# Talking-heads attention with a gated MLP: the row maxima and reciprocal sums of two softmax groups taken in shared instructions

## Chip, cores and metric

The kernel runs on one core of a Trainium2 chip. The metric is the time of one execution in device microseconds (us); lower is better. Engines are named as in the profile: PE is TensorE (PEld its weight loads), DVE VectorE, ACT ScalarE, POOL GpSimd, SP the engine that issues most transfers.

## What is computed

The inputs are q, k, v of shape (4 batches, 12 heads, 448 positions, 64), two 12x12 head-mixing matrices, and the weights of a gated MLP. Cut to what matters, with float32 throughout:

```python
scores = q @ k.transpose(0, 1, 3, 2) / sqrt(64)
scores = einsum('bhij,hg->bgij', scores, w_pre)           # mix heads before the softmax
attn = exp(scores - max(scores, -1))
attn = attn / (sum(attn, -1) + 1e-9)
attn = einsum('bhij,hg->bgij', attn, w_post)              # mix heads after it
x = (attn @ v).transpose(0, 2, 1, 3).reshape(4, 448, 768)
h = gelu(x @ w_in); u, v = halves of h
v = layer_norm(v) * g_ln; v = w_sg @ v + b_sg             # mixes positions
out = x + (u * v) @ w_out
```

## The kernel before, in words

**Groups.** The queries of a batch are cut into four chunks of 120, 120, 120 and 88. A group is 10 query rows of a chunk with all 12 heads, that is 120 rows laid on the partitions, with the 448 key positions along the free dimension. There are 12, 12, 12 and 9 groups in a batch's chunks, 180 in all. Two neighbouring groups of a chunk make a pair: 88 pairs have two groups, and one pair in each batch's fourth chunk has one, so that there are 92 pairs. The second and the fourth chunk of a batch run backwards, from their last group to their first.

**The way of a pair.** The scores of a chunk (`qk`, L643) are evacuated to SBUF (L302, L669), written to DRAM by SP and read back pair by pair (`load_pair`, L740), so that the heads of ten queries lie on the partitions. `premix` (L745) multiplies by the first mixing matrix on PE: 8 fp32 matmuls for the first chunk, 12 fp16 ones (high and low parts) for the others, for both groups of the pair in turn. Each group's result lies in a PSUM tile of its own, one bank of 2 KB a partition, from the pool `ps_s2` with two buffers.

**The way of a group.** `slot` (L863) then runs each group by itself: the row maximum with its sign turned (`softmax_max`, L775, DVE, reads PSUM); the exponential with its row sum (`softmax_exp`, L782, ACT, reads PSUM, and a second ACT instruction that reads out the sum); the reciprocal of the sum (`norm_r`, L787 and L788, two DVE instructions on one column); then, for the 45 groups of batch 0 ("full" groups), the second mixing matrix scaled by the reciprocal (`w_norm`, tile `wp`, one or two POOL instructions), and 8 fp32 matmul passes of PE (`postmix`, L830). For the 135 others, p is scaled (`p_norm`), split into an fp16 high part (`p_hi`) and low part (`p_lo`), mostly on POOL, and multiplied with the second mixing matrix in fp16 (L840). `postmix` writes into one bank of the two-bank tile `at2`; the result is evacuated (`postmix_hi`, L855, by the helper at L302) to SBUF. `av` (L951) multiplies with v, and the MLP units (L983 and around) follow as PE has room. p lies in one of three buffers (`p32p`), freed by the `postmix` of a full group and by `p_lo` otherwise.

**What sets the order.** The order in which every engine runs its instructions is written out in advance by a planner (`Plan`, L187) with a clock for each engine. Each step is a generator that yields engine, cost in ns, a rank, the time at which its input is there, and conditions on buffers; `run` (L239) takes the step that can start first, by rank among those within 100 ns of it. A result counts as usable 200 ns after its step ends (`LAT`). Engines with several possible places for a step (`p_norm`, evacuations) are chosen by the planner's clocks. Ranks are group numbers with offsets: `premix` n-3.5, maximum n-3, exponential n-2.5, reciprocal n-2, `postmix` n. The next `premix` is allowed once both exponentials of the pair before are planned (L768). Engines run their instructions in this order without overtaking; the planned times are estimates and the real waits are those of semaphores.

**Other users of the two banks.** In the start, `tr_bank` (L1296) gives transposes a bank of `at2` and a tile of `ps_s2` in turn. In the last batch `any_bank` (L1005) lets the MLP's units use the banks of `ps_s2` and `at2` beside its own two.

Of the kernel before, what the change touches and what calls it, by code (L numbers as in the profile page):

```python
# [9 lines left out]
F32 = mybir.dt.float32  # L10
# [3 lines left out]
AF = mybir.ActivationFunctionType  # L14
ALU = mybir.AluOpType
AX = mybir.AxisListType
PSUM = bass.MemoryType.PSUM
# [63 lines left out]
def talking_heads_gmlp(ctx, tc, q, k, v, w_pre, w_post, w_in, g_ln, w_sg, b_sg, w_out, out):  # L81
    nc = tc.nc
    B, H, S, D = q.shape
# [3 lines left out]
    P = 128  # L87
# [36 lines left out]
    p32p = ctx.enter_context(tc.tile_pool(name="p32p", bufs=3))  # L124
    wpp = ctx.enter_context(tc.tile_pool(name="wpp", bufs=2))
    dram = ctx.enter_context(tc.tile_pool(name="dram", bufs=1, space=DRAM))
    ps_s2 = ctx.enter_context(tc.tile_pool(name="ps_s2", bufs=2, space=PSUM))
    ps_at = ctx.enter_context(tc.tile_pool(name="ps_at", bufs=1, space=PSUM))
    ps_wk = ctx.enter_context(tc.tile_pool(name="ps_wk", bufs=2, space=PSUM))
    ps_ml = ctx.enter_context(tc.tile_pool(name="ps_ml", bufs=2, space=PSUM))  # L130
# [14 lines left out]
    wpc_hi = const.tile([P, H * NH], F16, name="wpc_hi")  # L145
    wpc_lo = const.tile([P, H * NH], F16, name="wpc_lo")
    at2 = ps_at.tile([P, 2, 512], F32, name="at2")
    p_ring = [[const.tile([P, (NC - 1) * TC + P], F16, name=f"p{w}{i}") for i in range(3)] for w in "hl"]
    neg_half = const.tile([P, 1], F32, name="neg_half")
    wv_hi = const.tile([P, KK, DH], F16, name="wv_hi")  # L150
# [36 lines left out]
    class Plan:  # L187
# [22 lines left out]
        def past(self, name, n):  # L210
            return 0 if n < 0 else self.tm.get((name, n))

        @staticmethod
        def after(times):
            return None if None in times else max(times)
# [78 lines left out]
    pl = Plan()  # L294
# [450 lines left out]
    def premix(p):  # L745

        i, t, n = pairs_[p]
        g = gring[p % RING]  # L750
        ns = sorted((m for m in range(n, min(n + 2, NG)) if pair_of[m] == p), key=lambda m: glist[m][2])
        for m in sorted(ns):
            st[m] = {"s2": ps_s2.tile([P, 512], F32, tag="s2", name="ps_s2")}
        if i < N_Q32:
            terms = (wpre32, g_full(p)),
        else:
            terms = (wpre_hi, g[:, :, 0]), (wpre_hi, g[:, :, 1]), (wpre_lo, g[:, :, 0])
        for k, (w, x) in enumerate(terms):
            for u, m in enumerate(ns):
                for f in range(2):  # L760
                    o, rows = 64 * (f ^ u), slice(64 * f, 64 * f + NH * H)
                    nc.tensor.matmul(st[m]["s2"][o:o + 64, :S], lhsT=w[rows], rhs=x[rows, u, :],  # L762
                                     start=(k == 0), stop=(k == len(terms) - 1))
        return sorted(ns)

    def all_premix():
        for p, (i, _, n) in enumerate(pairs_):
            t = yield "pe", 1500 if i < N_Q32 else 570, n - 3.5, 0, lambda: after([seen(("pair", p)), past("exp", n - 1), past("exp", n - 2)])  # L768
            for m in premix(p):
                tm["pre", m] = t  # L770
                pl.add(slot(m, t))

    def softmax_max(n):
        nm = small.tile([P, 1], F32, tag="nm", name="nm")
        nc.vector.tensor_reduce(out=nm, in_=st[n]["s2"][:, :S], axis=AX.X, op=ALU.max, negate=True)  # L775
        st[n]["nm"] = nm

    def softmax_exp(n):
        x = st[n]
        x["p32"] = p32p.tile([P, S], F32, tag="p32", name="p32")  # L780
        x["ss"] = small.tile([P, 1], F32, tag="ss", name="ss")
        nc.scalar.activation(out=x["p32"], in_=x["s2"][:, :S], func=AF.Exp, bias=x["nm"], accum_out=x["ss"])  # L782

    def norm_r(n):
        x = st[n]
        x["rs"] = small.tile([P, 1], F32, tag="rs", name="rs")
        nc.vector.tensor_scalar(out=x["rs"], in0=x["ss"], scalar1=1e-9, scalar2=1.0 / S_P, op0=ALU.add, op1=ALU.mult)  # L787
        nc.vector.reciprocal(out=x["rs"], in_=x["rs"])  # L788

    def w_norm(n):  # L790
        x = st[n]
# [71 lines left out]
    def slot(n, t):  # L863
        b, c, _ = glist[n]
        i = NCH * b + ORD.index(c)
        t = yield "dve", 531, n - 3, t
        softmax_max(n)
        t = yield "act", 611, n - 2.5, t, lambda: after([past("exp", n - 1), past("p32", n - 3)])
        softmax_exp(n)
        tm["exp", n] = t  # L870
        t = yield "dve", 300, n - 2, t, lambda: past("r", n - 1)
        norm_r(n)
        tm["r", n] = t
        full = n < N_F32 and (n < N_FULL or n * P_F32 % 1 < P_F32 or ck["pe"] < max(ck["dve"], ck["pool"]) + C_F32)
        if full:
            t = yield None, W_NORM[n < N_W], n - 1, t, lambda: after([past("ph", n - 1), past("post", n - 2)])
# [128 lines left out]
    def any_bank(b):  # L1005


        pool, tag = ps_ml, "ml"
        if b == B - 1:
            spare[0] += 1  # L1010
            pool, tag = ((ps_ml, "ml"), (ps_s2, "s2"), (None, "at"))[spare[0] % 3]
        if tag == "ml":
            name = bank()
        else:
            name = f"{tag}{spare[0] // 3 % 2}"
            if tag == "at":
                k = spare[0] // 3 % 2
                return name, lambda: at2[:, k]
        return name, lambda: pool.tile([P, 512], F32, tag=tag, name="ps_x")

    def gelu(ps, rows, cols, out, view, ml, done, need, last=True):

# [230 lines left out]
    with tc.manual_schedule():  # L1253
# [41 lines left out]

        def tr_bank():  # L1296
            turns[0] += 1
            if turns[0] % 2 == 0:
                return ps_s2.tile([P, 512], F32, tag="s2", name="ps_tr")
            return at2[:, turns[0] // 2 % 2]  # L1300

        def turned(part, e):
            src, oh, ol = part
# [123 lines left out]
```

## Time and profile before

| what | us |
|---|---|
| median of 3 runs | 637.63 |
| lowest and highest of them | 634.28, 639.41 |
| the profiled execution: its own time | 637.85 |
| the profiled execution: its span, first to last instruction | 636.1 |

Times in the rows below are us from the span's start, unless marked ns. "A <- B" in a row of waits says that A's engine sat idle until B ended. A row of the timeline has the start, the duration, the engine, the line, the operation and its tiles, and in square brackets the engine's idle time before it with what ended it; a number with x behind it counts merged instructions, and then the duration runs from the first one's start to the last one's end. PEclk is the granted clock of TensorE as a share of its full 2.4 GHz.

### The profile page before, as it was taken

The numbers are of one execution on the slowest core, as the hardware profiler recorded it, in microseconds if no ns is written. First come the engines' busy times: TensorE is split into PE (matmuls) and PEld (weight loads), VectorE is DVE, ScalarE is ACT, GpSimd is POOL, SyncE is SP. The second block draws the span as 40 slices with busy tenths as digits, with TensorE's granted clock in tenths as the row PEclk, the third lists the DMA queues.
The fourth block names the chain that finished last, engine by engine and source line by source line (L and its number), as shares of the span: only waits on it lengthen the run. The fifth ranks groups of instructions, "written<-read, shape, count | busy, mean of one in ns | idle before, by whom it ended". The sixth has DMA issues, their size and how long they took to land.

```text
span 636.1 us, 22960 instructions
## 1 busy us (share of the span) xinstructions
PE 587.2 (92%) x9305; PEld 389.0 (61%) x9305; DVE 451.8 (71%) x1093; ACT 451.8 (71%) x1038; POOL 385.4 (61%) x557
## 2 busy tenths in 40 slices
PE   7777879779999899999999999999999999999997
PEld 3234647557665665766676665667566746677764
DVE  5747678794899888676779979665788787544570
ACT  5646567666858779798769769787888778876332
POOL 4213553477577968786667968664697677866000
PEclk9878999989999699999999999999899999999999
DMA  9899498787488875769488747575697456440002
GB/s 220 230 254 304 125 285 212 187 219 195 125 247 252 210 185 145 195 178 268 126 246 205 203 111 192 150 201 163 181 239 214 130 149 170 134 113 4 3 1 88
DMA packets 79412, 112.22 MB, mean 176 GB/s; under 512 B 29290, under 2 KB 65802, under 8 KB 79306
## 3 DMA queue, kind: packets, MB, share of 16 engines
q1 hardware_dynamic: 79046, 110.74, 64.5%
q8 instruction: 73, 1.20, 0.8%
q14 instruction: 33, 0.27, 0.1%
q10 hardware_dynamic: 260, 0.01, 0.0%
HBM read 66.00 MB, written 44.73 MB: 174 GB/s over the span
## 4 chain that ended last, share of the span: by engine, by line
PE 57%; DVE 16%; ACT 9%; DMA 8%; issue 5%; POOL 4%; SPq 0%; POOLq 0%; ACTq 0%; DVEq 0%
PE ps_x L983 9%; PE ps_av L951 9%; PE ps_s L762 7%; PE ps_u L983 6%; PE ps_qk L643 6%; PE ps_v L983 6%; PE at L840 5%; PE at L830 4%; DVE s L669 4%; DVE nm L775 4%; ACT at L302 2%; ACT p L782 2%; DMA q<-in_q_dram 2%; DMA xTl<-in_moe_w_in_dram 2%; ACT s L302 2%
## 5 line engine op out<-in xcount | busy, mean ns | idle before, releaser
L302 ACT ACTIVATE at<-at 112x480 f32<-112x480 f32 x179 | 110.1, 616 | 43.7 <-PE at L830 23.2
L307 POOL TENSOR_TENSOR pl<-p,ph 128x448 f16<-128x448 f32 x127 | 133.4, 1054 | 8.7 <-ACT ph L302 4.2
L782 ACT ACTIVATE p<-ps_s,nm 128x448 f32<-128x448 f32 x180 | 114.1, 635 | 26.5 <-DVE nm L775 25.9
L775 DVE TENSOR_REDUCE nm<-ps_s 128x1 f32<-128x448 f32 x180 | 105.3, 615 | 31.6 <-PE ps_s L762 30.4
L669 DVE SCALAR_TENSOR_TENSOR s<-ps_qk,s 120x448 f16<-120x448 f32 (+1 forms) x172 | 100.5, 615 | 18.0 <-ACT s L302 16.3
L304 POOL TENSOR_SCALAR p<-p,rs 128x448 f32<-128x448 f32 x87 | 56.4, 649 | 66.1 <-DVE rs L788 27.5
L302 ACT ACTIVATE s<-ps_qk 120x448 f16<-120x448 f32 (+2 forms) x158 | 79.0, 544 | 12.2 <-PE ps_qk L643 10.4
L643 PE MATMUL ps_qk<-kT,qT 64*128 64x448 f16 (+1 forms) x576 | 79.0, 362 | 7.5 <-DVE s L669 2.6
L840 PEld LDWEIGHTS <-ph 64*128 64x128 f16 x2160 | 53.7, 94 | 40.2 <-issue 24.6
L951 PE MATMUL ps_av<-at,v 112*64 112x120 f32 (+1 forms) x1536 | 77.4, 260 | 0.7 <-ACT at L302 0.7
L951 PEld LDWEIGHTS ps_av<-at,v 112*64 112x64 f32 x1536 | 74.0, 137 | 4.3 <-issue 1.8
L304 POOL TENSOR_SCALAR wp<-wpost,rs 128x60 f32<-128x60 f32 (+1 forms) x64 | 27.2, 436 | 72.4 <-DVE rs L788 53.7
L830 PE MATMUL at<-wp,p 128*112 128x120 f32 x360 | 50.5, 288 | 20.6 <-ACT at L302 10.0
L983 PE MATMUL ps_u<-xTh,wbuf 128*128 128x128 f16 (+1 forms) x768 | 66.9, 217 | 0.4 <-DVE gbuf L1039 0.4
L840 PE MATMUL at<-wpc_hi,ph 64*128 64x60 f16 x1080 | 62.0, 190 | 5.5 <-ACT at L302 4.7
L983 PEld LDWEIGHTS <-wbuf 128*128 128x128 f16 x1152 | 60.5, 100 | 7.4 <-issue 5.7
L830 PEld LDWEIGHTS at<-wp,p 128*112 128x112 f32 x360 | 43.0, 189 | 34.1 <-POOL wp L304 17.1
L304 POOL TENSOR_SCALAR ph<-p 128x448 f16<-128x448 f32 x89 | 50.8, 571 | 18.3 <-ACT xTh L302 6.8
L983 PE MATMUL ps_u<-xTl,wbuf 128*128 128x128 f16 (+1 forms) x384 | 61.8, 216 | 0.0
L840 PE MATMUL at<-wpc_hi,pl 64*128 64x60 f16 x1080 | 60.6, 188 | 0.8 <-DVE rs L787 0.5
L840 PE MATMUL at<-wpc_lo,ph 64*128 64x60 f16 x1080 | 61.0, 188 | 0.0
L983 PE MATMUL ps_x<-wo,gbuf 128*128 128x384 f16 (+1 forms) x336 | 56.6, 328 | 0.0
(214 smaller groups left out, 1176.5 us busy)
## 6 DMA issues: line engine op xcount, KB each, us to landing
g<-s_d SPq DMA_DIRECT2D x176, 210.0 KB, 4.4
s_d<-s SPq DMA_DIRECT2D x62, 420.0 KB, 3.9
s_d<-s SPq DMA_DIRECT2D x24, 336.0 KB, 3.4
v<-in_v_dram SPq DMA_DIRECT2D x12, 448.0 KB, 7.3
out_dram<-ot SPq DMA_DIRECT2D x24, 192.0 KB, 2.9
q<-in_q_dram SPq DMA_DIRECT2D x11, 384.0 KB, 5.3
st<-in_k_dram SPq DMA_DIRECT2D x9, 448.0 KB, 5.0
st<-in_moe_w_out_dram SPq DMA_DIRECT2D x8, 384.0 KB, 4.3
```

The costliest lines, as they stand in the source:

```text
L302: e.activation(out=o, in_=i, func=AF.Copy, scale=scale)
L304: e.tensor_scalar(out=o, in0=i, scalar1=scale, scalar2=1.0, op0=ALU.mult, op1=ALU.mult)
L307: (e or pl.on).tensor_tensor(out=o, in0=a, in1=b, op=ALU.subtract)
L643: nc.tensor.matmul(ps[:rows, :S], lhsT=qT2[i % 2][r, tq, h // 2, :rows], rhs=kT[r, h // HG, tk, h // 2 % 2, :], start=(n == 0), stop=(n == 2))
L669: nc.vector.scalar_tensor_tensor(out=e[:ev, h % 2, 1, :], in0=ps[:ev, :S], scalar=1.0 / math.sqrt(D), in1=e[:ev, h % 2, 0, :], op0=ALU.mul ...
L762: nc.tensor.matmul(st[m]["s2"][o:o + 64, :S], lhsT=w[rows], rhs=x[rows, u, :], start=(k == 0), stop=(k == len(terms) - 1))
L775: nc.vector.tensor_reduce(out=nm, in_=st[n]["s2"][:, :S], axis=AX.X, op=ALU.max, negate=True)
L782: nc.scalar.activation(out=x["p32"], in_=x["s2"][:, :S], func=AF.Exp, bias=x["nm"], accum_out=x["ss"])
L830: nc.tensor.matmul(ps[:TC, jc * w:(jc + 1) * w], lhsT=x["p32"][:, jc * TC:(jc + 1) * TC], rhs=x["wp"], start=True, stop=True)
L840: nc.tensor.matmul(at2[:, hf ^ glist[n][2] % 2, jc * w:(jc + 1) * w], lhsT=l[rows, js], rhs=r[rows], start=(k == 0), stop=(k == 2))
L951: nc.tensor.matmul(ps[a * D:(a + 1) * D, k3 * rows:(k3 + 1) * rows], lhsT=x[:, h, jc, :], rhs=y[:, jc, h, w:w + rows], start=(jc == 0 and ...
L983: nc.tensor.matmul(o, lhsT=l, rhs=r, start=first, stop=last)
```

## The change

The two score tiles of a pair become the two banks of one tile `s2`, which is allotted once. One DVE instruction takes the maxima of both groups (128 partitions x 2 x 448 in, 128 x 2 out), after `premix` of the pair. Two exponentials follow as before, each with its own column of the maxima and of the sums. The addition with its scaling, and the reciprocal, are then done once for the pair on two columns, after the second exponential; only then do the two groups go their own ways in `slot`. The planner's costs are 60 + 475 ns a group for the maxima, 635 for an exponential (611 before) and 270 for the reciprocals of the pair (300 a group before). `tr_bank` and `any_bank` use the banks of `s2`.

```diff
--- before.py
+++ after.py
@@ -124,7 +124,7 @@
     p32p = ctx.enter_context(tc.tile_pool(name="p32p", bufs=3))
     wpp = ctx.enter_context(tc.tile_pool(name="wpp", bufs=2))
     dram = ctx.enter_context(tc.tile_pool(name="dram", bufs=1, space=DRAM))
-    ps_s2 = ctx.enter_context(tc.tile_pool(name="ps_s2", bufs=2, space=PSUM))
+    ps_s2 = ctx.enter_context(tc.tile_pool(name="ps_s2", bufs=1, space=PSUM))
     ps_at = ctx.enter_context(tc.tile_pool(name="ps_at", bufs=1, space=PSUM))
     ps_wk = ctx.enter_context(tc.tile_pool(name="ps_wk", bufs=2, space=PSUM))
     ps_ml = ctx.enter_context(tc.tile_pool(name="ps_ml", bufs=2, space=PSUM))
@@ -145,6 +145,7 @@
     wpc_hi = const.tile([P, H * NH], F16, name="wpc_hi")
     wpc_lo = const.tile([P, H * NH], F16, name="wpc_lo")
     at2 = ps_at.tile([P, 2, 512], F32, name="at2")
+    s2 = ps_s2.tile([P, 2, 512], F32, name="s2")
     p_ring = [[const.tile([P, (NC - 1) * TC + P], F16, name=f"p{w}{i}") for i in range(3)] for w in "hl"]
     neg_half = const.tile([P, 1], F32, name="neg_half")
     wv_hi = const.tile([P, KK, DH], F16, name="wv_hi")
@@ -749,8 +750,8 @@
         i, t, n = pairs_[p]
         g = gring[p % RING]
         ns = sorted((m for m in range(n, min(n + 2, NG)) if pair_of[m] == p), key=lambda m: glist[m][2])
-        for m in sorted(ns):
-            st[m] = {"s2": ps_s2.tile([P, 512], F32, tag="s2", name="ps_s2")}
+        for u, m in enumerate(ns):
+            st[m] = {"u": u}
         if i < N_Q32:
             terms = (wpre32, g_full(p)),
         else:
@@ -759,33 +760,38 @@
             for u, m in enumerate(ns):
                 for f in range(2):
                     o, rows = 64 * (f ^ u), slice(64 * f, 64 * f + NH * H)
-                    nc.tensor.matmul(st[m]["s2"][o:o + 64, :S], lhsT=w[rows], rhs=x[rows, u, :],
+                    nc.tensor.matmul(s2[o:o + 64, u, :S], lhsT=w[rows], rhs=x[rows, u, :],
                                      start=(k == 0), stop=(k == len(terms) - 1))
         return sorted(ns)
 
     def all_premix():
         for p, (i, _, n) in enumerate(pairs_):
             t = yield "pe", 1500 if i < N_Q32 else 570, n - 3.5, 0, lambda: after([seen(("pair", p)), past("exp", n - 1), past("exp", n - 2)])
-            for m in premix(p):
-                tm["pre", m] = t
-                pl.add(slot(m, t))
-
-    def softmax_max(n):
-        nm = small.tile([P, 1], F32, tag="nm", name="nm")
-        nc.vector.tensor_reduce(out=nm, in_=st[n]["s2"][:, :S], axis=AX.X, op=ALU.max, negate=True)
-        st[n]["nm"] = nm
-
-    def softmax_exp(n):
-        x = st[n]
-        x["p32"] = p32p.tile([P, S], F32, tag="p32", name="p32")
-        x["ss"] = small.tile([P, 1], F32, tag="ss", name="ss")
-        nc.scalar.activation(out=x["p32"], in_=x["s2"][:, :S], func=AF.Exp, bias=x["nm"], accum_out=x["ss"])
-
-    def norm_r(n):
-        x = st[n]
-        x["rs"] = small.tile([P, 1], F32, tag="rs", name="rs")
+            ns = premix(p)
+            tm.update({("pre", m): t for m in ns})
+            pl.add(pair_slot(p, ns, t))
+
+    def pair_slot(p, ns, t):
+
+        a = min(ns)
+        x = {}
+        for k in ("nm", "ss", "rs"):
+            x[k] = small.tile([P, 2], F32, tag=k, name=k)[:, :len(ns)]
+        t = yield "dve", 60 + 475 * len(ns), a - 3, t
+        nc.vector.tensor_reduce(out=x["nm"], in_=s2[:, :len(ns), :S], axis=AX.X, op=ALU.max, negate=True)
+        for n in sorted(ns):
+            t0 = yield "act", 635, n - 2.5, t, lambda: after([past("exp", n - 1), past("p32", n - 3)])
+            u = st[n]["u"]
+            st[n]["p32"] = p32p.tile([P, S], F32, tag="p32", name="p32")
+            nc.scalar.activation(out=st[n]["p32"], in_=s2[:, u, :S], func=AF.Exp, bias=x["nm"][:, u:u + 1],
+                                 accum_out=x["ss"][:, u:u + 1])
+            tm["exp", n] = t0
+        t = yield "dve", 270, a - 2, t0
         nc.vector.tensor_scalar(out=x["rs"], in0=x["ss"], scalar1=1e-9, scalar2=1.0 / S_P, op0=ALU.add, op1=ALU.mult)
         nc.vector.reciprocal(out=x["rs"], in_=x["rs"])
+        for n in sorted(ns):
+            st[n]["rs"] = x["rs"][:, st[n]["u"]:st[n]["u"] + 1]
+            pl.add(slot(n, t))
 
     def w_norm(n):
         x = st[n]
@@ -863,14 +869,6 @@
     def slot(n, t):
         b, c, _ = glist[n]
         i = NCH * b + ORD.index(c)
-        t = yield "dve", 531, n - 3, t
-        softmax_max(n)
-        t = yield "act", 611, n - 2.5, t, lambda: after([past("exp", n - 1), past("p32", n - 3)])
-        softmax_exp(n)
-        tm["exp", n] = t
-        t = yield "dve", 300, n - 2, t, lambda: past("r", n - 1)
-        norm_r(n)
-        tm["r", n] = t
         full = n < N_F32 and (n < N_FULL or n * P_F32 % 1 < P_F32 or ck["pe"] < max(ck["dve"], ck["pool"]) + C_F32)
         if full:
             t = yield None, W_NORM[n < N_W], n - 1, t, lambda: after([past("ph", n - 1), past("post", n - 2)])
@@ -1005,18 +1003,16 @@
     def any_bank(b):
 
 
-        pool, tag = ps_ml, "ml"
+        tag = "ml"
         if b == B - 1:
             spare[0] += 1
-            pool, tag = ((ps_ml, "ml"), (ps_s2, "s2"), (None, "at"))[spare[0] % 3]
+            tag = ("ml", "s2", "at")[spare[0] % 3]
         if tag == "ml":
             name = bank()
         else:
-            name = f"{tag}{spare[0] // 3 % 2}"
-            if tag == "at":
-                k = spare[0] // 3 % 2
-                return name, lambda: at2[:, k]
-        return name, lambda: pool.tile([P, 512], F32, tag=tag, name="ps_x")
+            k = spare[0] // 3 % 2
+            return f"{tag}{k}", lambda: (s2 if tag == "s2" else at2)[:, k]
+        return name, lambda: ps_ml.tile([P, 512], F32, tag=tag, name="ps_x")
 
     def gelu(ps, rows, cols, out, view, ml, done, need, last=True):
 
@@ -1295,9 +1291,7 @@
 
         def tr_bank():
             turns[0] += 1
-            if turns[0] % 2 == 0:
-                return ps_s2.tile([P, 512], F32, tag="s2", name="ps_tr")
-            return at2[:, turns[0] // 2 % 2]
+            return (s2, at2)[turns[0] % 2][:, turns[0] // 2 % 2]
 
         def turned(part, e):
             src, oh, ol = part
```

## Rows read from the trace of the kernel before

**Rows 1.** The page, part 1: busy time, share of the span, instructions.
```profile
span 636.1 us, 22960 instructions
...
PE 587.2 (92%) x9305; PEld 389.0 (61%) x9305; DVE 451.8 (71%) x1093; ACT 451.8 (71%) x1038; POOL 385.4 (61%) x557
```

**Rows 2.** Windows: busy us of PE, PEld, DVE, ACT, POOL; PEclk, DMA share, GB/s.
```profile
25.00:170.00 145.00, 118.98 (x1207) 81.78 (x1203) 102.95 (x267) 91.13 (x218) 69.34 (x120) 0.92 0.81 221
170.00:300.00 130.00, 123.59 (x2122) 80.46 (x2122) 107.97 (x255) 105.42 (x242) 100.76 (x130) 0.96 0.75 204
300.00:578.00 278.00, 270.90 (x5220) 182.43 (x5215) 202.26 (x502) 221.68 (x518) 200.99 (x265) 0.99 0.63 170
578.00:636.00 58.00, 54.57 (x654) 36.44 (x652) 24.28 (x42) 19.23 (x35) 6.65 (x13) 1.00 0.07 25
```

**Rows 3.** The page, part 4: the chain that ended last.
```profile
PE 57%; DVE 16%; ACT 9%; DMA 8%; issue 5%; POOL 4%; SPq 0%; POOLq 0%; ACTq 0%; DVEq 0%
PE ps_x L983 9%; PE ps_av L951 9%; PE ps_s L762 7%; PE ps_u L983 6%; PE ps_qk L643 6%; PE ps_v L983 6%; PE at L840 5%; PE at L830 4%; DVE s L669 4%; DVE nm L775 4%; ACT at L302 2%; ACT p L782 2%; DMA q<-in_q_dram 2%; DMA xTl<-in_moe_w_in_dram 2%; ACT s L302 2%
```

**Rows 4.** Groups of DVE instructions, shapes apart: xcount | busy us, mean ns.
```profile
L775 DVE TENSOR_REDUCE nm<-ps_s 128x1 f32<-128x448 f32 x180 | 105.3, 615 | 31.6 <-PE ps_s L762 30.4
...
L788 DVE RECIPROCAL rs<-rs 128x1 f32<-128x1 f32 x180 | 29.5, 164 | 6.2
...
L787 DVE TENSOR_SCALAR rs<-ss 128x1 f32<-128x1 f32 x180 | 26.5, 147 | 28.1 <-ACT p L782 26.8
...
L1033 DVE SCALAR_TENSOR_TENSOR gl_a<-gl_a,ps_v 128x512 f32<-128x512 f32 x12 | 8.2, 686 | 10.0 <-ACT gl_a L1030 9.8
...
L1033 DVE SCALAR_TENSOR_TENSOR gl_a<-gl_a,ps_v 128x256 f32<-128x256 f32 x4 | 1.6, 411 | 0.5 <-ACT gl_a L1030 0.5
```

**Rows 5.** Waits from 25 to 170 us: total us, times, longest us.
```profile
POOL wp L304 <- DVE rs L788: 53.7, 23, 12.1
...
PEld at L830 <- POOL wp L304: 17.1, 14, 3.2
...
PE at L830 <- ACT at L302: 9.1, 12, 1.8
PE at L830 <- POOL wp L304: 8.8, 7, 2.8
...
PEld ps_s L762 <- ACT p L782: 5.1, 4, 2.0
```

**Rows 6.** Timeline, one pair of groups: start us, us, instruction.
```profile
66.38 1.16 DVE L775 TENSOR_REDUCE nm<-ps_s 128x1 f32<-128x448 f32 x2 [2.20 <-PE ps_s L762]
...
68.11 0.16 DVE L788 RECIPROCAL rs<-rs 128x1 f32<-128x1 f32 x1
68.27 0.62 ACT L782 ACTIVATE p<-ps_s,nm 128x448 f32<-128x448 f32 x1
...
68.47 1.02 POOL L304 TENSOR_SCALAR wp<-wpost,rs 128x60 f32<-128x60 f32 x2 [4.14 <-DVE rs L788]
...
69.39 0.16 DVE L788 RECIPROCAL rs<-rs 128x1 f32<-128x1 f32 x1
...
69.59 1.05 PE L830 MATMUL at<-wp,p 128*112 128x120 f32 x8 [1.55 <-POOL wp L304]
69.75 0.63 POOL L304 TENSOR_SCALAR wp<-wpost,rs 128x120 f32<-128x120 f32 x1 [0.26 <-DVE rs L788]
...
70.67 0.57 ACT L302 ACTIVATE at<-at 112x480 f32<-112x480 f32 x1 [0.36 <-PE at L830]
...
71.39 1.04 PE L830 MATMUL at<-wp,p 128*112 128x120 f32 x8 [0.75 <-ACT at L302]
```

**Rows 7.** Timeline from 53 us: two postmixes and their first evacuation.
```profile
53.69 1.86 PE L830 MATMUL at<-wp,p 128*112 128x120 f32 x16
...
55.59 0.58 ACT L302 ACTIVATE at<-at 112x480 f32<-112x480 f32 x1 [0.86 <-PE at L830]
```

**Rows 8.** Timeline of the start: turning keys and queries.
```profile
7.37 0.61 DVE L307 TENSOR_TENSOR kT<-ps_tr,kT 128x448 f16<-128x448 f32 x1
...
7.89 0.49 PE L324 MATMUL ps_tr<-ident,q 128*128 128x128 f32 x3
```

## Prediction

> **What bounds the kernel now.** I read the page's busy shares first, then windows by stage, then the chain, then the waits of the stage in which PE idles. DVE is busy for 71% of the span, PE for 92% [rows 1]. The windows show where the other 8% lie [rows 2]: PE is idle for 145 - 119.0 = 26.0 us between 25 and 170 us (batch 0, the full groups), but only 6.4 of 130 us from there to 300, 7.1 of 278 us to 578, and 3.4 us in the tail, which has no softmax. From 170 us on, then, the end is set by PE's own work, and a faster DVE can win back at most some 13 us there. The chain agrees: 57% of it is PE and 16% DVE, of which the row maximum is 4% of the span, about 25 us [rows 3]. In the first stage PE waits mostly for the softmax chain: 17.1 + 8.8 = 25.9 us in 21 waits for `wp`, the mixing weights scaled by the reciprocal, and POOL in turn sits 53.7 us waiting for that reciprocal; 9.1 us more go to waits for an evacuation of `at2` [rows 5].
>
> **The maxima.** 180 DVE instructions of 615 ns become 88 on two banks and 4 on one. The trace has no two-bank reduction. From PSUM, 512 columns take 686 ns and 256 take 411 [rows 4], a slope of 1.07 ns a column, so the double one should take 0.615 + 448 x 1.07 ns = 1.10 us. Two back to back take 1.16 us today [rows 6], two apart 1.23. Its ends are 0.615 us (the second bank free) and 1.23 us (nothing shared); per pair that is a relief of 0.55 us down to a loss of 0.07, for 88 pairs 48 us to -6 us of DVE time. I take 1.10, the slope of the nearest rows: 88 x 0.06 = 5 us.
>
> Those rows say that little is left to save: in the back-to-back pair the second maximum adds 1.16 - 0.615 = 0.545 us, of which 448 x 1.07 = 0.48 is the columns themselves [rows 4, 6]. The Trainium skill (Perfetto Trace Analysis, Optimizing Scalar/DVE Operations) puts the engine-busy overhead of a DVE instruction on PSUM at about 125 ns. By that figure the 88 dropped instructions would give 11 us of DVE time, by the rows 5; the sum goes by the rows.
>
> **The reciprocals.** 360 instructions become 184: 88 pairs of instructions of 147 + 164 ns [rows 4] go, 88 x 0.311 = 27 us of DVE time. The second column should cost a nanosecond or so by the slope above; at the other end, two columns for the price of two instructions, nothing is saved. I take 27. DVE's relief is then 5 + 27 = 32 us of 451.8, to about 420 us (66% of the span).
>
> **What reaches the end.** Little of it, because PE is full where most of the groups run. If 32 of 452 us left the chain's DVE share evenly, 16% of 636 = 102 us would lose 102 x 0.07 = 7 us. PE's idle time from 170 us on is 13.5 us in all, and PE's own work takes over where a DVE stretch leaves the chain; I count half of the 7, 3.5 us. The planner sees a DVE clock that is 2 x (531 + 300) - (1010 + 270) = 382 ns lighter a pair and an ACT clock 48 ns heavier, so it may hand a few evacuations to DVE; I cost that at nothing, since ACT and POOL are busy for some 80% or less of the windows [rows 2]. Where they were needed, it would cost up to the DVE time just won.
>
> **What comes later.** The first group of a pair now waits for its partner twice: its exponential starts 1.10 - 0.615 = 0.5 us later, and its reciprocal comes after the second exponential. In the pair shown, the first reciprocal starts at 68.11 and the second at 69.39 [rows 6]: 1.28 us later for the first group, about nothing for the second. Queued behind the waiting reciprocal on DVE are evacuations of the scores and pieces of the weights' preparation; for `wp` POOL waits, for that PE. From 170 us on PE has other work; in batch 0 it hasn't always. The same rows show what comes back. PE's postmix of the first group waits for `wp` until 69.59; the second group's `wp` is ready at 70.38, but its postmix starts at 71.39, just after the first one's evacuation (70.67 to 71.24). The other case is two postmixes back to back, after which the first evacuation starts only at 55.59 although the pair of postmixes began at 53.69 and half of the 1.86 us would have done [rows 7]. Writes to one bank of `at2` and reads of the other thus never overlap here; the order planned decides who waits. With both groups released by one reciprocal, their scaled weights come one `wp` apart (0.63 and 1.02 us in these rows), no more than a postmix takes, and the planner should put the two postmixes back to back. The first would then start near 70.6 instead of 69.59 and the second end near 72.5, against 71.39 + 1.04 = 72.43 now. So +0.1 us a pair, and for batch 0's 23 pairs between -0.6 (where the evacuation's wait goes and the delay is hidden by a matmul of another kind) and +1.28 us each, or -14 to +29 us. I take 0 to +2, say +1 us.
>
> **One tile for two banks.** The lesson of `at2` holds for `s2`: a `premix` may not write one bank while the other is read. But the planner lets it start only after both exponentials, and its matmuls take both groups in turn, so waiting for the second instead of the first moves it by no more than PE waits here today, 5.1 us in 4 waits [rows 5]; I count 0, at most +5. In the start, the second transpose into the pool's tiles at 7.89 would wait for the reader of the first, which ends at 7.98 [rows 8]: +0.1 us. In the tail `s2`'s two banks alternate with four others, so the earlier one is read out by then; 0.
>
> **The sum.** 637.85 (the profiled execution, whose 1.75 us outside the span stay) - 3.5 + 1 + 0.1 = 635.4; 637.85 lies 0.2 above the median of the runs, so I forecast 635.
>
> **Rivals.** *Faster: DVE's stretches end the stage.* Between 100 and 300 us DVE is the busiest beside PE (108 of 130 us in the second window [rows 2]); if there each pair's 0.06 + 0.31 = 0.37 us came off the end, 33 pairs would give 12 us, and 625 would result; with the postmixes pulled together in batch 0 as well, less. For it speaks DVE's share of the chain, against it PE's 95% in that window. Chance 0.28.
>
> *Slower: the first group's delay in batch 0.* If the planner finds no other matmul for PE while `wp` is late, half of the 21 waits for `wp`, those for a pair's first group, grow by 1.28 us, some 13 us, and 651 results; it decides from the point where the reciprocal comes later than PE's filler ends, which today is already the case in these 21 waits. Against it speaks the evacuation wait that falls away. The Trainium skill (same page and section) has the rule for this side: where a vector engine isn't saturated but causes bubbles on others, breaking up instructions may let work finish sooner; this change does the reverse on an engine that is 71% busy. Chance 0.22.
>
> *No effect:* PE covers both the relief and the delay, and only the reshuffled order shows, 637. Chance 0.20; the forecast itself has 0.30.
>
> **How the numbers follow.** The measurement can tell about 1% from no change, so "same" is 631 to 644. The forecast and the rival of no effect lie inside, the two others outside: faster 0.28, same 0.50, slower 0.22. The range reaches to both outer rivals without their tails: 623 to 649. The forecast's own range is 631 to 641.
>
> **What would show it.** Right, if the new maximum takes 1.05 to 1.15 us, 92 pairs of reciprocals stay near 0.31 us each, DVE's busy time falls to about 420 us, PE's busy time stays near 587, the waits of PE for an evacuation of `at2` shrink while those for `wp` grow, and the stretch to 170 us keeps its length within 3 us. Wrong, if PE's idle time between 25 and 170 us leaves 20 to 32 us, if the double maximum costs over 1.2 us, or if a stage past 300 us, in which PE now is 97% busy, changes its length by more than 5 us.

## The result, and the profile after

The changed kernel took 648.44 us (median of 4 runs, 646.45 to 650.42) beside 637.73 us (634.28 to 639.41): a ratio of 1.015, interval 1.0112 to 1.0187. It is slower by 1.5%. The profiled execution took 646.45 us with a span of 644.7.

The page's part 1 of the kernel after, which answers to [rows 1]:

```profile
span 644.7 us, 22550 instructions
...
PE 591.6 (92%) x9305; PEld 393.5 (61%) x9305; DVE 433.7 (67%) x829; ACT 463.4 (72%) x1067; POOL 369.7 (57%) x528
```

The span grew by 8.6 us: 4.2 us are idle time of PE (644.7 - 591.6 = 53.1, against 48.9), 4.4 us are PE's busy time with the same 9305 matmuls. DVE lost 264 instructions and 18.1 us. ACT has 29 instructions more than in [rows 1] and POOL 29 fewer: the new plan also moved work between engines, above all the scaling of p, its high parts and `wp`. "Order" below thus means where an instruction runs as well as when. The windows of the kernel after (columns as in [rows 2], the last one longer) show where PE idles:

```profile
25.00:170.00 145.00, 119.14 (x1212) 83.92 (x1209) 99.77 (x201) 94.02 (x230) 65.41 (x113) 0.90 0.81 221
170.00:300.00 130.00, 120.01 (x1987) 77.54 (x1986) 97.94 (x182) 100.40 (x231) 90.79 (x117) 0.95 0.69 189
300.00:578.00 278.00, 270.35 (x5122) 181.53 (x5122) 192.90 (x368) 227.21 (x525) 188.93 (x244) 0.99 0.66 176
578.00:644.00 66.00, 62.33 (x881) 41.99 (x877) 28.65 (x51) 27.22 (x56) 16.94 (x24) 1.00 0.07 23
```

Batch 0, where I had looked for the loss, lost nothing: PE is idle for 25.9 us up to 170, as before (26.0). From there to 300 us it idles for 10.0 instead of 6.4 us, and to 578 for 7.7 instead of 7.1. The granted clock of the first two windows is 0.02 and 0.01 lower, which stretches PE's work by about 119 x 0.02 + 120 x 0.01 = 3.6 us (an estimate from rounded shares), most of the 4.4. It is no cause by itself: another execution of the changed kernel, with a mean clock of 0.979 instead of 0.963, took 647.93 us.

The chain that ended last in the kernel after, against [rows 3], shows DVE's share down from 16 to 14%, the maximum's part of it from 4 to 2%, and the DMA's down from 8 to 3%; PE's rose from 57 to 64%:

```profile
PE 64%; DVE 14%; ACT 10%; issue 4%; DMA 3%; POOL 3%; POOLq 0%; ACTq 0%; DVEq 0%
PE ps_av L949 11%; PE ps_x L981 8%; PE ps_u L981 7%; PE s L763 7%; PE at L846 7%; PE ps_qk L644 6%; PE ps_v L981 6%; PE at L836 5%; DVE s L670 3%; ACT p L786 3%; ACT at L303 2%; ACT s L303 2%; DVE nm L781 2%; DVE rs L790 1%; PE s L981 1%
```

The new instructions, in the groups of DVE of the kernel after (columns as in [rows 4]):

```profile
L781 DVE TENSOR_REDUCE nm<-s 128x2 f32<-128x896 f32 x88 | 95.5, 1086 | 31.4 <-PE s L763 30.4
...
L790 DVE TENSOR_SCALAR rs<-ss 128x2 f32<-128x2 f32 x88 | 22.3, 253 | 41.3 <-ACT p L786 41.1
...
L791 DVE RECIPROCAL rs<-rs 128x2 f32<-128x2 f32 x88 | 14.6, 166 | 3.0
```

The double maximum takes 1.086 us. The pair of reciprocals takes 253 + 166 = 419 ns, not 311. And the waits from 25 to 170 us of the kernel after, against [rows 5]:

```profile
POOL wp L305 <- DVE rs L791: 58.5, 18, 12.4
...
PEld at L836 <- POOL wp L305: 11.7, 14, 1.4
...
PE s L763 <- ACT p L786: 7.0, 7, 2.3
...
PEld s L763 <- ACT p L786: 5.7, 2, 3.1
...
PE at L836 <- ACT at L303: 4.0, 7, 0.8
PE at L836 <- POOL wp L305: 3.5, 7, 1.0
```

PE's waits for `wp` fell from 25.9 to 15.2 us; those for `at2`'s evacuation fell too (9.1 to 4.0 on PE); what came instead is `premix` waiting for the exponential, 7.0 + 5.7 = 12.7 us instead of 7.2 (5.1 on PEld [rows 5] and 2.1 on PE, a line shown with onetile below). Last, the softmax as a whole ends later. The line of the exponential (min/median/max ns, first and last start), of the kernel before and of the kernel after:

```profile
L782 ACT ACTIVATE p<-ps_s,nm x180: 609/634/705, 25.9 to 576.5; 128x448 f32<-128x448 f32 x180
```
```profile
L786 ACT ACTIVATE p<-s,nm x180: 612/634/713, 26.5 to 592.2; 128x448 f32<-128x448 f32 x180
```

The last one starts 15.7 us later, more than the 8.6 us of the span.

### The profile page after: what moved, and what is told of

Its sections match the earlier page's. It is cut to its first block, busy times and chain, and to the rows that moved or that the text cites. A ratio compares the mean times of both kernels' runs of the same rounds, so it can differ in the third digit from the quotient of the medians.

```text
span 644.7 us, 22550 instructions
## 1 busy us (share of the span) xinstructions
PE 591.6 (92%) x9305; PEld 393.5 (61%) x9305; DVE 433.7 (67%) x829; ACT 463.4 (72%) x1067; POOL 369.7 (57%) x528
## 4 chain that ended last, share of the span: by engine, by line
PE 64%; DVE 14%; ACT 10%; issue 4%; DMA 3%; POOL 3%; POOLq 0%; ACTq 0%; DVEq 0%
PE ps_av L949 11%; PE ps_x L981 8%; PE ps_u L981 7%; PE s L763 7%; PE at L846 7%; PE ps_qk L644 6%; PE ps_v L981 6%; PE at L836 5%; DVE s L670 3%; ACT p L786 3%; ACT at L303 2%; ACT s L303 2%; DVE nm L781 2%; DVE rs L790 1%; PE s L981 1%
## 5 line engine op out<-in xcount | busy, mean ns | idle before, releaser
L303 ACT ACTIVATE at<-at 112x480 f32<-112x480 f32 x178 | 109.7, 616 | 46.8 <-PE at L836 25.1
L786 ACT ACTIVATE p<-s,nm 128x448 f32<-128x448 f32 x180 | 113.8, 634 | 14.9 <-DVE nm L781 12.9
L781 DVE TENSOR_REDUCE nm<-s 128x2 f32<-128x896 f32 (+1 forms) x92 | 98.0, 1066 | 32.8 <-PE s L763 31.6
L305 POOL TENSOR_SCALAR p<-p,rs 128x448 f32<-128x448 f32 x71 | 46.3, 652 | 82.5 <-DVE rs L791 31.0
L949 PE MATMUL ps_av<-at,v 112*64 112x120 f32 (+1 forms) x1536 | 79.6, 264 | 3.8 <-DVE s L670 2.7
L949 PEld LDWEIGHTS ps_av<-at,v 112*64 112x64 f32 x1536 | 75.8, 139 | 8.4 <-issue 3.0
L981 PE MATMUL ps_u<-xTh,wbuf 128*128 128x128 f16 (+1 forms) x768 | 69.1, 217 | 0.7 <-DVE gbuf L1035 0.7
L836 PE MATMUL at<-wp,p 128*112 128x120 f32 x360 | 52.7, 297 | 9.8 <-ACT at L303 4.0
L836 PEld LDWEIGHTS at<-wp,p 128*112 128x112 f32 x360 | 45.0, 196 | 24.3 <-POOL wp L305 11.7
L305 POOL TENSOR_SCALAR ph<-p 128x448 f16<-128x448 f32 x77 | 44.0, 572 | 20.0 <-ACT xTh L303 7.9
L763 PE MATMUL s<-g,wpre_hi 60*64 60x448 f16 x672 | 50.2, 363 | 5.4 <-ACT p L786 2.9
```

Source lines behind the costliest of these rows:

```text
L303: e.activation(out=o, in_=i, func=AF.Copy, scale=scale)
L305: e.tensor_scalar(out=o, in0=i, scalar1=scale, scalar2=1.0, op0=ALU.mult, op1=ALU.mult)
L763: nc.tensor.matmul(s2[o:o + 64, u, :S], lhsT=w[rows], rhs=x[rows, u, :], start=(k == 0), stop=(k == len(terms) - 1))
L781: nc.vector.tensor_reduce(out=x["nm"], in_=s2[:, :len(ns), :S], axis=AX.X, op=ALU.max, negate=True)
L786: nc.scalar.activation(out=st[n]["p32"], in_=s2[:, u, :S], func=AF.Exp, bias=x["nm"][:, u:u + 1], accum_out=x["ss"][:, u:u + 1])
L836: nc.tensor.matmul(ps[:TC, jc * w:(jc + 1) * w], lhsT=x["p32"][:, jc * TC:(jc + 1) * TC], rhs=x["wp"], start=True, stop=True)
```

## The experiments

Each ratio is to the kernel before, run beside it on the same chip. In the order in which they came up, the theories were: the sharing makes data late (the first group's exponential and reciprocal); the written order of the engines, which the planner draws anew; p's buffers, held longer; the one tile for two banks; and luck of the order, by which any order differs from the next. Letters in the quoted expectations are the names that these theories had at the time.

| kernel | PSUM tiles | maxima / reciprocals | order | ratio [95%] | span |
|---|---|---|---|---|---|
| after | one | joint / joint | its own | 1.0150 [1.0112, 1.0187] | 644.7 |
| order_single | one | single / single | after's | 1.0127 [1.0060, 1.0194] | 642.7 |
| early_rs | one | single / single, first one early | after's | 1.0100 [1.0069, 1.0131] | 641.1 |
| order_single_tt | two | single / single | after's | 1.0092 [1.0058, 1.0126] | 639.8 |
| after_costs | one | joint / joint | second | 1.0037 [1.0003, 1.0071] | 638.1 |
| after_costs2 | one | joint / joint | third | 1.0014 [0.9983, 1.0045] | 640.1 |
| after_late | one | joint / joint | fourth | 1.0055 [1.0024, 1.0085] | 642.3 |
| maxonly | one | joint / single | its own | 0.9975 [0.9936, 1.0015] | 638.0 |
| maxonly_costs | one | joint / single | second | 1.0082 [1.0050, 1.0114] | 639.3 |
| rsonly | one | single / joint | its own | 1.0195 [1.0139, 1.0252] | 646.5 |
| rs_twotile | two | single / joint | rsonly's | 0.9950 [0.9924, 0.9975] | 634.4 |
| rs_twotile_b | two | single / joint | rsonly's | 0.9947 [0.9918, 0.9975] | 631.7 |
| rs_tt_costs | two | single / joint | second | 0.9900 [0.9869, 0.9932] | 634.5 |
| onetile | one | single / single | before's | 1.0267 [1.0222, 1.0312] | 655.9 |
| order_joint | one | joint / single | before's | 1.0205 [1.0159, 1.0251] | 649.0 |
| costs | two | single / single | a second of before's | 0.9991 [0.9947, 1.0035] | 634.2 |
| before_buf4 | two | single / single | with 4 buffers of p | 1.0057 [1.0029, 1.0085] | 639.4 |
| after_buf4 | one | joint / joint | with 4 buffers of p | 1.0042 [1.0007, 1.0076] | 640.9 |
| rsonly_buf4 | one | single / joint | with 4 buffers of p | 1.0354 [1.0321, 1.0387] | 658.7 |

**Is it the shared instructions?** order_single keeps the order of the kernel after on every engine but lets each shared instruction be two of one group again, at the same place.

```diff
-        nc.vector.tensor_reduce(out=x["nm"], in_=s2[:, :len(ns), :S], axis=AX.X, op=ALU.max, negate=True)
+        for n in sorted(ns):
+            u = st[n]["u"]
+            nc.vector.tensor_reduce(out=x["nm"][:, u:u + 1], in_=s2[:, u, :S], axis=AX.X, op=ALU.max, negate=True)
...
-        nc.vector.tensor_scalar(out=x["rs"], in0=x["ss"], scalar1=1e-9, scalar2=1.0 / S_P, op0=ALU.add, op1=ALU.mult)
-        nc.vector.reciprocal(out=x["rs"], in_=x["rs"])
+        for n in sorted(ns):
+            one_rs(x, st[n]["u"])
```

> The changed kernel's written order on every engine, but each shared DVE instruction is split again: two maxima of 448 columns back to back, and two one-column pairs of reciprocal instructions, still after the second exponential. Theory A (the wait for the partner and the order planned around it make the loss): ratio to the kernel before 1.012 to 1.022, no faster than the changed kernel, DVE busy near 450 us. Theory B (the shared instructions themselves cost, the double maximum above all): back to 0.995 to 1.005.

early_rs is the same, with the first group's reciprocal issued between the two exponentials.

> As order_single, but the first group's reciprocal stands in DVE's order ahead of the second exponential, so that only data can hold its followers; PE, ACT, POOL and SP keep the changed kernel's order. Theory A1 (the late reciprocal itself holds POOL and then PE): most of the loss goes, ratio 0.998 to 1.008, and PE's waits for pl fall to the 3 us of before. Theory A2 (the planned order makes the loss, whenever the data are there): ratio 1.010 to 1.020 and PE's idle time unchanged.

The page's part 1 of order_single:

```profile
span 642.7 us, 22825 instructions
...
PE 586.4 (91%) x9305; PEld 388.1 (60%) x9305; DVE 447.4 (70%) x1093; ACT 463.0 (72%) x1067; POOL 370.6 (58%) x528
```

1.0127 and 1.0100 beside 1.0150: with 13.7 us more DVE work (447.4 against 433.7) and the same order, nothing is slower. So the sharing's relief of DVE is worth nothing that can be measured, and the late reciprocal costs at most some tenths of a per cent; the intervals of the three ratios are 0.3 to 0.7% wide to either side. Most of the loss sits in what these kernels have in common with the kernel after: the order and the tile.

**Each half alone.** maxonly shares only the maxima, rsonly only the reciprocals; both keep the one tile and are planned anew.

```diff
 maxonly
         nc.vector.tensor_reduce(out=x["nm"], in_=s2[:, :len(ns), :S], axis=AX.X, op=ALU.max, negate=True)
...
+        for n in ns:
+            pl.add(slot(n, t, x))
 rsonly
+            tmax[n] = yield "dve", 531, n - 3, t
+            nc.vector.tensor_reduce(out=x["nm"][:, u:u + 1], in_=s2[:, u, :S], axis=AX.X, op=ALU.max, negate=True)
```

> One joint maximum a pair, but exponentials, reciprocals and all that follows by group as before, order planned anew with the costs of before. Theory A (the joined reciprocal makes the loss): ratio 0.993 to 1.005. Theory B (the joint maximum makes it): 1.010 to 1.020.

> Maxima by group (two instructions), the reciprocals joined after the second exponential as in the changed kernel, order planned anew. Theory A: ratio 1.010 to 1.022, with waits of PE for pl as in the changed kernel. Theory B: 0.995 to 1.005.

0.9975 and 1.0195: the halves don't add up, and the one with the single maxima is the slow one. At this point both the joined reciprocals and the one tile could be its cause.

**Buffers and the planner's costs.** after_buf4 and before_buf4 have a fourth buffer of p, costs has the kernel before with 505, 635 and 135 ns as the planner's costs of maximum, exponential and reciprocal.

```diff
-    p32p = ctx.enter_context(tc.tile_pool(name="p32p", bufs=3))
+    p32p = ctx.enter_context(tc.tile_pool(name="p32p", bufs=4))
```

> The changed kernel with a fourth buffer for p, so that the second exponential of a pair waits for a group one earlier. Theory C (the joined reciprocal holds two of three buffers of p before either group can go on, so exponentials, reciprocals and POOL's splitting take turns, and the order planned around it makes the loss): most of the loss goes, ratio 0.995 to 1.006. Theory D (the delay of the first group and the two groups going on in step make the loss, whatever the buffers): 1.010 to 1.020.

> Control: the kernel before with a fourth buffer for p. Theory C: by group, three buffers were enough, ratio 0.995 to 1.003. If a fourth buffer helps any order alike, it is faster here too, 0.985 to 0.992.

> The kernel before with only the planner's costs of the changed one (505, 635 and 135 ns a group for maximum, exponential and reciprocal): no instruction changes, only the order. Theory E (any new order costs or gains a per cent): 0.99 to 1.02, away from 1. Theories C and D: 0.996 to 1.004.

costs, only a new order, left the kernel before where it was (0.9991). The fourth buffer, which brings a new order too, seemed to help the kernel after (1.0042), but it made the kernel before slower (1.0057). rsonly_buf4 puts it into the kernel with the joined reciprocals alone:

> Maxima by group, joined reciprocals, one two-bank tile (the run that gave 1.0195), now with a fourth buffer for p. Theory C (the joined reciprocal is short of buffers): the loss falls by over 1%, ratio 0.998 to 1.008. Theory E (luck of an order): it stays anywhere, 1.00 to 1.02, and as likely above 1.012 as below.

1.0354, against 1.0195 with three buffers: the fourth buffer did not take the loss away. Since this too is another order, the theory of buffers falls for good only with rs_twotile (below), which has three buffers and no loss. What after_buf4 gained, after_costs gained without a buffer (below), so that the new order is enough to account for it.

**The one tile alone.** onetile is the kernel before, same instructions in the same written order; only the two score tiles become banks of one (which the transposes of the start and the MLP's units of the last batch then use as well).

```diff
-            st[m] = {"s2": ps_s2.tile([P, 512], F32, tag="s2", name="ps_s2")}
+            st[m] = {"s2": s2[:, u], "u": u, "ns": len(ns), "first": m == min(ns)}
```

> The kernel before, same written order and same instructions, only with the two banks of the scores in one tile, so that a premix waits for both exponentials before it writes either bank. Theory F (one tile for two banks is a large part of the loss): 1.008 to 1.018, PE's waits for the exponential up from 2 to 7 us or more. Otherwise 0.998 to 1.004.

1.0267, the largest effect of any single edit here with three buffers. Two maxima and the first exponential, in the timeline of the kernel before and of onetile:

```profile
195.75 1.14 DVE L775 TENSOR_REDUCE nm<-ps_s 128x1 f32<-128x448 f32 x2
...
196.58 0.63 ACT L782 ACTIVATE p<-ps_s,nm 128x448 f32<-128x448 f32 x1
```
```profile
193.88 1.16 DVE L776 TENSOR_REDUCE nm<-s 128x1 f32<-128x448 f32 x2 [0.46 <-PE s L763]
...
195.15 0.63 ACT L783 ACTIVATE p<-s,nm 128x448 f32<-128x448 f32 x1 [2.77 <-DVE nm L776]
```

Before, ACT reads the first bank from 196.58 on, while DVE reads the second until 195.75 + 1.14 = 196.89. In onetile ACT starts at 195.15, after the second maximum's end at 195.04, although it needs only the first, which ended some 0.5 us sooner. The waits of the whole run, of the kernel before and of onetile (total us, times, longest):

```profile
DVE rs L787 <- ACT p L782: 26.8, 57, 1.3
ACT p L782 <- DVE nm L775: 25.9, 31, 2.7
...
PEld ps_s L762 <- ACT p L782: 5.1, 4, 2.0
...
PE ps_s L762 <- ACT p L782: 2.1, 2, 1.2
```
```profile
ACT p L783 <- DVE nm L776: 48.3, 50, 3.3
DVE rs L788 <- ACT p L783: 41.3, 77, 1.3
...
PE s L763 <- ACT p L783: 7.5, 7, 3.6
PEld s L763 <- ACT p L783: 7.1, 2, 4.0
...
DVE nm L776 <- ACT p L783: 6.3, 12, 0.8
```

ACT's wait for a maximum nearly doubles, and a wait of a new kind appears: the second maximum waits for the first exponential, 12 times. Both are reads, of different banks. It isn't these two places alone: in the whole trace of the kernel before, 68 of the 180 maxima run at the same time as an exponential, 24.6 us together; in onetile, and in every other kernel here with one tile, none does. So the program's semaphores follow the tile, not the bank, and hold a reader back for a reader. The Trainium skill (PSUM — Partial Sum Buffer, PSUM bank collisions raise a hardware error) asks for a guard by bank and quadrant of partitions, reads against reads included, and calls accesses to different banks clean. The overlap in the kernel before agrees with it; the one tile guards more than that rule wants.

rs_twotile makes the same point from the other side: the order of rsonly, with two tiles.

> The written order of the run with joined reciprocals and maxima by group (1.0195), but with two score tiles as before. Theory F: most of the loss goes, 1.000 to 1.008. Theory C: it stays, 1.013 to 1.022.

0.9950 against 1.0195, the same instructions in the same order. PE's idle time falls in every stage; the windows of rsonly and of rs_twotile to 578 us:

```profile
25.00:170.00 145.00, 113.34 (x1195) 80.31 (x1192) 100.29 (x221) 91.10 (x223) 63.43 (x110) 0.92 0.83 224
170.00:300.00 130.00, 121.33 (x2020) 77.10 (x2021) 103.02 (x211) 104.77 (x240) 91.20 (x120) 0.97 0.72 192
300.00:578.00 278.00, 268.14 (x5065) 177.37 (x5066) 196.63 (x412) 224.03 (x514) 187.47 (x241) 0.99 0.64 175
```
```profile
25.00:170.00 145.00, 119.47 (x1208) 82.54 (x1205) 101.62 (x224) 93.08 (x228) 65.48 (x113) 0.92 0.83 225
170.00:300.00 130.00, 124.16 (x2129) 80.37 (x2131) 103.55 (x214) 107.02 (x246) 93.29 (x120) 0.97 0.75 202
300.00:578.00 278.00, 272.13 (x5231) 180.40 (x5228) 200.65 (x425) 226.99 (x526) 191.77 (x248) 1.00 0.63 170
```

By stage PE is idle for 31.7, 8.7 and 9.9 us with one tile and 25.5, 5.8 and 5.9 us with two: 13.0 us in all, beside 12.1 us of span. The joined reciprocals, without the tile, cost nothing; in this order the kernel rather gains. rs_twotile_b, the same kernel measured again, gave 0.9947.

> The run rs_twotile again, measured in more rounds: 0.992 to 0.998 if it beats the kernel before, 0.998 to 1.002 if that was chance.

order_joint is onetile with the joint maximum at the first group's place.

> The kernel before in its own order, but with the scores in one two-bank tile and the joint maximum at the place of the first group's; reciprocals by group. It shows what the shared maximum alone is worth without a new order. If DVE's time decides anywhere: 0.992 to 0.998. If it decides nowhere, and one tile for two banks costs nothing: 0.998 to 1.003. If the one tile costs: over 1.005.

1.0205: in an order that was planned for two readings, the joint maximum is nearly as dear as the guard that it replaces.

**What the tile costs in the order of the kernel after.** order_single_tt is order_single with two tiles.

> The changed kernel's written order on PE, ACT, POOL and SP and its late reciprocals, with single-group DVE instructions (the run order_single, 1.0127), but with two score tiles as before. Theory F (one tile for two banks makes the changed kernel's loss): 0.990 to 1.003, PE's waits for the exponential at a premix back to 5 us or less. Theory G (the order with the late first group makes it): 1.008 to 1.018.

1.0092 against 1.0127, intervals that overlap: here the tile costs some 0.35%, perhaps nothing. The order of the kernel after has the two maxima as one block and both exponentials behind it, so that less is left for the guard to hold up: with two tiles only 30 of the 180 maxima run beside an exponential in this order (9.8 us together), against 68 in the order of the kernel before. The 1.0092 is the written order alone, with the places of the instructions and the late reciprocals that belong to it: instructions of one group and two tiles, as before.

**Other orders.** after_costs and after_costs2 are the kernel after with other planner's costs for maxima, exponential and reciprocals (1062, 611 and 300; 1060, 660 and 330 ns, instead of 1010, 635 and 270). They do the same work; the planner writes it in another order, and places a few instructions on other engines (DVE, ACT and POOL run 829, 1067 and 528 in the kernel after, and 824, 1074 and 526 in after_costs). after_late lets the planner count on `premix` 400 ns later.

```diff
-        t = yield "dve", 60 + 475 * len(ns), a - 3, t
+        t = yield "dve", 531 * len(ns), a - 3, t
```

> The changed kernel, planned with other costs (1062 ns for a double maximum, 611 for an exponential, 300 for the reciprocals), so in another order. Theories C and F: the loss stays whatever the order, 1.009 to 1.021. Theory E: it may land anywhere from 0.995 to 1.02.

> The changed kernel in a third order (planner's costs 1060, 660 and 330 ns). If the change costs about a per cent in itself and the rest of 1.015 is the order drawn: 1.002 to 1.013. If it costs 1.5% in itself and the second order (1.0037) was the lucky one: 1.012 to 1.022. If the change costs nothing in itself: as likely below 1 as above.

> The changed kernel, whose planner is told that a premix may start only 400 ns after the planned end of both exponentials, so that other matmuls come first. If PE's waits of 7 us for the exponential make a good part of the loss: 1.000 to 1.009, with those waits down to 3 us. If they only stand in for other waits: 1.008 to 1.018.

1.0037, 1.0014 and 1.0055 where the change as given has 1.0150. In after_late the waits of `premix` for the exponential (PE alone) fall from 7.3 to 2.6 us over the run, which gained no more than any other redrawing did. maxonly and rs_twotile were drawn a second time as well:

> The joint maximum over one tile, reciprocals by group (the run maxonly, 0.9975), planned with 635 and 270 ns in place of 611 and 300, so in another order. If the joint maximum pays for the one tile in any order: 0.994 to 1.004. Theory E: 1.004 to 1.015, as the changed kernel in its two orders.

> Joined reciprocals, maxima by group, two tiles (the run rs_twotile, 0.995), planned with 611 and 300 ns in place of 635 and 270, so in another order. Theory F: 0.990 to 1.004, no loss in any order. Theory E (luck of the order): up to 1.015.

maxonly went from 0.9975 to 1.0082, rs_twotile from 0.9950 to 0.9900, the best kernel of all: 633.42 us beside 638.89. Between orders of the same work the ratios thus differ by 1.4% (the kernel after, four orders), 1.1% (maxonly), 0.5% (rs_twotile) and 0.1% (the kernel before, against costs): in some cases as much as what was to be measured.

## Why the prediction was wrong, point by point

The forecast was 635 us, with 631 to 641 as its own range; 648.44 lies within the wide range (to 649), on the side that had a chance of 0.22, but not by that rival's mechanism: that the wide range holds it is luck.

- **The failed step is the planner's order, which the sum took at nothing.** For the work that the planner would place elsewhere I counted nothing, and the rival of no effect had the reshuffling at nothing too. The drawn order alone measured 0.92% (order_single_tt, 1.0092 [1.0058, 1.0126], some 6 us) of the 1.5%. It did not hand DVE more to do, as I had thought possible, but moved 29 instructions from POOL to ACT. The change in three other orders came to 1.0014 to 1.0055. So of the 1.5%, about 1% belongs to this one draw, and the change itself costs between nothing and some 0.6%, as far as four orders can tell. What in that order loses is open: the 3.6 us of idle time between 170 and 300 us and the later end of the softmax locate it, no more. PE, its weight loads apart, waits 5.4 us for the low parts `pl` in the kernel after and 3.5 us in order_single_tt, and never in the kernel before; but in rs_tt_costs, the fastest, it waits 4.0 us for them, so that these waits don't decide it alone.
- **"One tile for two banks", counted at 0, at most +5, failed as well**, though it is the smaller part here. By itself the tile measured 2.67% (onetile, 17 us) and 2.5% (rsonly against rs_twotile, 16 us), in orders that weren't planned for it. I had weighed only `premix` against the two readings, there with PEld's 5.1 us and without PE's own 2.1 us, and missed the readings against each other, though [rows 7] already showed one tile's banks waiting for each other. In the changed kernel the joint maximum makes that wait part of the work, and an order planned for it hides most of it: the tile is worth some 0.35% there (1.0127 against 1.0092, not resolved).
- **The maxima** were right: 1.086 us for 1.10; the groups' busy time fell from 105.3 to 95.5 + 2.5 (the four single ones) = 98.0 us, 7.3 us for 5 predicted. The Trainium skill's 125 ns (Perfetto Trace Analysis, Optimizing Scalar/DVE Operations), 11 us by that figure, lies above what was measured, the rows' 5 us below it.
- **The reciprocals** were mis-sized: 419 ns a pair for 311; the groups' busy time fell from 56.0 to 22.3 + 14.6 us and some 1.3 us for the four single ones, 17.8 us of relief instead of 27. The second column's "nanosecond or so" was right for the reciprocal (166 against 164 ns) and wrong for the addition (253 against 147), see below. DVE's busy time fell by 18.1 us instead of 32, and by less than the 7.3 + 17.8 = 25.1 us of the groups. Its other 553 instructions didn't grow (331 us in both kernels, added up one by one). But the records of neighbouring instructions overlap, by 46 us in the kernel before and by 33 in the kernel after, so that an instruction that goes frees less than it lasts.
- **What reaches the end**, 3.5 us, was too much: order_single gives the relief back and is no slower. That PE sets the end from 170 us on was right.
- **What comes later**: predicted +1 us for batch 0, where PE's idle time stayed the same (25.9 us, right). The fall of the waits for `at2` came as said; that the waits for `wp` would grow did not, they fell by 10.7 us. With that the slower rival fell as a mechanism, and early_rs against order_single (1.0100 against 1.0127) shows the late reciprocal itself to cost nothing that can be told. The Trainium skill's rule that breaking up instructions may let work finish sooner where a vector engine isn't saturated but causes bubbles on others (Perfetto Trace Analysis, Optimizing Scalar/DVE Operations) isn't borne out at this place: broken up in the same order, the time is the same within the intervals.
- **The faster rival** fell with the relief; only without the one tile does a part of the change gain clearly: 0.5 to 1.0% (rs_twotile, rs_tt_costs).

## What to carry to other kernels

In these kernels a tile is the unit of the program's waits: two banks in one tile are read and written in turn by different engines, reads too, so give each bank its own tile unless one instruction must span both. Relief of an engine that isn't the bound can be worth nothing: 13.7 us of DVE's time, given back in the same order, changed nothing that could be measured. Where a planner writes the order, every edit draws a new one, and here the draws of one kernel lay up to 1.4% apart: run an edit in two or three orders (the same work, other costs), and undo it in the edited kernel's own order, before crediting the edit.

## What the runs showed of the hardware that was not expected

The two-column addition takes 0.3 to 1.1 us at times. Its line in the kernel before and after (min/median/max ns), and one case in the timeline of the kernel after:

```profile
L787 DVE TENSOR_SCALAR rs<-ss x180: 121/153/156, 26.9 to 577.3; 128x1 f32<-128x1 f32 x180
```
```profile
L790 DVE TENSOR_SCALAR rs<-ss x92: 136/169/1104, 28.5 to 593.0; 128x2 f32<-128x2 f32 x88, 128x1 f32<-128x1 f32 x4
```
```profile
322.68 1.04 POOL L308 TENSOR_TENSOR pl<-p,ph 128x448 f16<-128x448 f32 x1
...
323.13 0.61 DVE L790 TENSOR_SCALAR rs<-ss 128x2 f32<-128x2 f32 x1 [0.17 <-ACT p L786]
```

DVE's instruction ends at 323.74, 0.02 us after POOL's at 323.72. Of the 92 in the kernel after, 15 take over 300 ns, and all 15 start while a POOL instruction runs; 14 end 0.02 to 0.03 us after it. In rs_twotile it is 18 of 18. Of the 15 other two-column additions that start beside a POOL instruction in the kernel after, nine meet its last 0.15 us and take the usual time, four end 0.02 us after it, and two, beside POOL instructions on a single column (`mv`), don't wait. The one-column form never takes over 156 ns in the kernel before, though 98 of its 180 start beside a running POOL instruction. The 15 take 10 us together, 7.4 us more than at the median of 169 ns, which is the whole excess of the mean. The Trainium skill (SBUF — State Buffer, SBUF: two separate sides) tells of a port pair that GpSimd shares with DVE's two-port modes as an exclusive lock, whose loser waits for the whole other instruction. These rows agree; that the second column is what makes the addition use that mode is argued from the two forms, and was not tried by itself.
